# A spectral filter beside a gated MLP on one core: the fifth column class joins the other four on VectorE, tile 3's statistics move to ScalarE, and the warm-up reads a constant

## The chip, the core and the metric

The kernel runs on one core of one Trainium2 chip. The core's engines run side by side and wait for each other through semaphores: TensorE multiplies matrices into PSUM (eight banks), VectorE and ScalarE work on elements and move results from PSUM to SBUF, GpSimd does small element work, and the sync engine issues transfers. The metric is the time of one execution on the device in microseconds (us), as the median of several runs. The profile's span is a little shorter, since it begins with the first instruction and ends with the last.

## The reference, cut to what matters

The input x has 2048 rows of 640 numbers in bf16. Three things are added:

```
xn  = layernorm(x)                              # over the 640 columns
A   = irfft2(rfft2(xn) * (w_r + 1j * w_i))      # over rows and columns; weights 2048 x 321
B   = ((xn @ w_gate) * (xn @ w_up)) @ w_down    # 640 -> 1536 -> 640
out = x + A + B
```

A is a product in the frequency domain: a two-dimensional real Fourier transform, a multiplication by 2048 x 321 complex weights, and the transform back. B is a gated MLP without a nonlinearity.

## The kernel before

Everything lies in one SBUF arena, cut into 16 tiles of 128 rows. The work falls into five stages that overlap.

1. *Layer norm and transposes.* Tiles 0 to 5 get their statistics on VectorE (`bn_stats`, lines 756 and 765), tiles 6 to 15 on ScalarE as a sum and a sum of squares (lines 738 and 747). Tiles 0 to 3 are transposed on TensorE (line 818), the others by transfers. Ahead of it TensorE runs 40 warm-up matmuls and later ten fill matmuls on a small buffer that VectorE sets to zero (lines 696, 709, 720).
2. *The first product of B (GU).* For 12 blocks of 128 hidden columns and for gate and up, five matmuls of 512 columns each (line 948; for the first tiles in smaller pieces, line 968). ScalarE or VectorE moves the result out of PSUM (lines 684 and 685, the copy helper that all evictions share), and VectorE multiplies gate and up (lines 984 and 985, called H). These units are also used as TensorE's filling further down.
3. *The first half of the transform.* VectorE does a radix-10 step over the columns of each tile (lines 860 to 895), TensorE the radix-64 step over rows (line 908, R).
4. *The stage that the change rewrites.* It goes over t = 0 to 15, two frequency groups q of 128 rows each. The 321 column frequencies fall into five classes by their rest modulo 5: four classes of 64 columns and a fifth, the multiples of 5, of 65 columns.
   - D (line 1025): two times five matmuls give real and imaginary parts by columns; eD evicts them in two pieces of 64 partitions each.
   - C (line 1045): two matmuls of 321 columns finish the row transform. Partitions 0 to 63 now hold real parts, 64 to 127 imaginary parts.
   - WM on VectorE: products with w_r and with w_i. Four instructions (line 1062) cover the four classes and go to the buffer PR, two (line 1068) cover the fifth class and go to the buffer Y5.
   - SM, after every second t (lines 1089 and 1090): differences and sums of these products, which complete the complex product for the four classes, go to the buffer L.
   - JA and JB (emitted through line 685 or 684, and through line 1101 or 684): copies of one half of the partitions to the other, one of them with the sign changed, so that L also holds i times the product. They may run on ScalarE or VectorE.
   - NS on GpSimd (lines 1077 to 1079): for the fifth class, two copies and a negation inside Y5.
   - IA (lines 1116 and 1118): the first inverse step for one q. Four matmuls of 64 columns, one for each class, read their weights from L at a step of four elements. The fifth class takes two matmuls that accumulate in PSUM, one for the products with w_r and one for those with w_i, with two different tables (`ti[..., 0]` and `ti[..., 1]`): there TensorE, not VectorE, completes the complex product. eIA evicts to SBUF.
5. *The inverse transform and the second product of B.* I (line 1147) is the inverse over columns on TensorE, V on VectorE the inverse radix-10 step (lines 1171 to 1204). ACC (line 1224) multiplies the hidden values with w_down into PSUM in two halves of 320 columns for each tile, 12 matmuls each, in pieces of five, four and three; IV (line 1236) adds the spectral part into the same bank; FIN adds x and the result is stored (lines 1245 and 1263).

The order of the work is written out. The kernel describes each piece of work as a task with its engine, the buffers it reads and writes and its PSUM bank. A long list, `_PLAN`, says in which order each engine takes the tasks, which engine takes those that may run on two, and which bank they use. A small function replays the list, finds which semaphores each task must wait for, and emits the instructions. Each engine takes its tasks strictly in this order. The numbers of nanoseconds that stand beside the tasks in the code are what the list was planned with; they do nothing on the chip.

The inverse tables TI lie under the w_down rows in the arena, so these rows can be loaded only once the IA that read the tables are done.

Of the kernel before, what the change touches and what calls it, by code (L numbers as in the profile page):

```python
# [255 lines left out]
def _build_tables():  # L256
# [65 lines left out]
    ti = np.zeros((128, _NQ, 2, 64), np.float64)  # L322
    for q in range(_NQ):
        k = _rows(q, npm, nk1)
        ph = two_pi * ((s1[:, None] * k[None, :]) % _S) / _S
        c = np.exp(-1j * ph)
        pm = np.broadcast_to(npm[None, :], (64, 64))
        f = np.where(ck == 1, np.where(pm == 1, -1j, 1j), 1.0 + 0j)
        if q == 0:
            f = (ck == pm).astype(np.complex128)  # L330
        fm = c * f
        im = (np.conj(c) * f / _S).T
        tf[0:64, q, n_re] = fm.real
        tf[0:64, q, n_im] = fm.imag
        tf[64:128, q, n_re] = -fm.imag
        tf[64:128, q, n_im] = fm.real
        ti[n_re, q, 0] = im.real
        ti[n_im, q, 0] = -im.imag
        ti[n_re, q, 1] = im.imag
        ti[n_im, q, 1] = im.real  # L340
# [21 lines left out]
_WD_LOADS = ((7, 12), (0, 2), (2, 4), (4, 6), (6, 7))  # L362
_FT_ORDER = (7, 8, 9, 10, 11, 0, 1, 2, 3, 4, 5, 6)
# [4 lines left out]
_LP = 321  # L368
_YS = 1090
_NY = 3  # L370
# [5 lines left out]
def _d_mm(n):  # L376
    return max(n, 64) / 2.4 + 2.5
# [22 lines left out]
def _d_act(n):  # L400
# [4 lines left out]
    (12, 4, -1), (0, 1, -1), (13, 4, -1), (176, 1, -1), (175, 4, -1), (8, 2, -1), (19, 2, -1), (9, 3, -1), (177, 4, -1),  # L405
    (18, 2, -1), (20, 2, -1), (11, 0, 0), (23, 2, -1), (21, 1, -1), (22, 2, -1), (24, 2, -1), (29, 2, -1), (25, 0, 2),
    (28, 2, -1), (26, 1, -1), (27, 2, -1), (178, 4, -1), (10, 0, 4), (14, 4, -1), (30, 2, -1), (33, 2, -1), (31, 1, -1),
    (32, 2, -1), (187, 0, 5), (34, 2, -1), (185, 0, 4), (188, 1, -1), (35, 0, 6), (15, 4, -1), (37, 2, -1), (192, 0, 5),
    (190, 0, 0), (186, 1, -1), (189, 2, -1), (38, 2, -1), (179, 4, -1), (36, 1, -1), (39, 2, -1), (180, 4, -1), (181, 4, -1),
    (197, 0, 1), (40, 2, -1), (48, 2, -1), (41, 1, -1), (43, 2, -1), (42, 2, -1), (193, 1, -1), (195, 0, 2), (44, 2, -1),  # L410
    (47, 2, -1), (202, 0, 3), (200, 0, 4), (182, 4, -1), (191, 1, -1), (196, 1, -1), (198, 1, -1), (49, 2, -1), (50, 1, -1),
    (16, 4, -1), (194, 2, -1), (201, 1, -1), (45, 0, 2), (52, 2, -1), (51, 2, -1), (183, 4, -1), (53, 2, -1), (207, 0, 6),
    (46, 1, -1), (184, 4, -1), (199, 2, -1), (118, 2, -1), (54, 0, 7), (205, 0, 2), (1, 4, -1), (203, 1, -1), (204, 2, -1),
    (55, 1, -1), (210, 0, 3), (212, 0, 7), (217, 0, 5), (208, 1, -1), (17, 4, -1), (215, 0, 4), (119, 2, -1), (206, 1, -1),
    (209, 2, -1), (120, 2, -1), (56, 2, -1), (211, 1, -1), (60, 2, -1), (59, 2, -1), (2, 4, -1), (3, 4, -1), (57, 2, -1),
    (68, 1, -1), (69, 1, -1), (213, 1, -1), (220, 0, 0), (121, 2, -1), (4, 4, -1), (58, 2, -1), (70, 1, -1), (216, 1, -1),
    (61, 2, -1), (218, 1, -1), (62, 1, -1), (122, 2, -1), (63, 2, -1), (222, 0, 1), (5, 4, -1), (214, 2, -1), (64, 2, -1),
    (125, 0, 2), (221, 1, -1), (71, 1, -1), (223, 1, -1), (123, 0, 6), (126, 1, -1), (219, 2, -1), (227, 0, 4), (127, 2, -1),
    (232, 0, 5), (225, 0, 0), (72, 1, -1), (230, 0, 1), (224, 2, -1), (128, 2, -1), (6, 4, -1), (7, 4, -1), (228, 1, -1),
    (66, 2, -1), (78, 1, -1), (79, 1, -1), (237, 0, 4), (226, 1, -1), (129, 2, -1), (235, 0, 0), (73, 2, -1), (80, 1, -1),  # L420
    (233, 1, -1), (229, 2, -1), (81, 1, -1), (130, 2, -1), (231, 1, -1), (82, 1, -1), (240, 0, 5), (76, 2, -1), (131, 2, -1),
    (238, 1, -1), (134, 0, 2), (74, 2, -1), (236, 1, -1), (83, 2, -1), (234, 2, -1), (242, 0, 4), (84, 2, -1), (65, 4, -1),
    (245, 0, 1), (67, 4, -1), (241, 1, -1), (75, 4, -1), (88, 1, -1), (77, 4, -1), (239, 2, -1), (135, 1, -1), (252, 0, 0),
    (247, 0, 5), (136, 2, -1), (243, 1, -1), (89, 1, -1), (244, 2, -1), (246, 1, -1), (132, 0, 2), (137, 2, -1), (90, 1, -1),
    (91, 1, -1), (86, 2, -1), (248, 1, -1), (250, 0, 1), (249, 2, -1), (255, 0, 4), (92, 1, -1), (98, 1, -1), (251, 1, -1),
    (85, 4, -1), (87, 4, -1), (437, 4, -1), (438, 4, -1), (93, 2, -1), (99, 1, -1), (138, 2, -1), (439, 4, -1), (253, 1, -1),
    (257, 0, 5), (256, 1, -1), (100, 1, -1), (258, 1, -1), (96, 2, -1), (254, 2, -1), (101, 1, -1), (139, 2, -1), (260, 0, 1),
    (262, 0, 0), (267, 0, 4), (94, 2, -1), (263, 1, -1), (133, 1, -1), (102, 1, -1), (261, 1, -1), (259, 2, -1), (140, 2, -1),
    (265, 0, 5), (103, 2, -1), (266, 1, -1), (440, 4, -1), (268, 1, -1), (270, 0, 0), (143, 0, 2), (264, 2, -1), (441, 4, -1),
    (104, 2, -1), (272, 0, 1), (124, 1, -1), (141, 0, 4), (269, 2, -1), (442, 4, -1), (108, 1, -1), (271, 1, -1), (273, 1, -1),  # L430
    (277, 0, 6), (149, 2, -1), (274, 2, -1), (109, 1, -1), (275, 0, 7), (280, 0, 0), (443, 4, -1), (142, 1, -1), (282, 0, 1),
    (444, 4, -1), (276, 1, -1), (278, 1, -1), (147, 0, 4), (281, 1, -1), (445, 4, -1), (145, 0, 6), (150, 2, -1), (446, 4, -1),
    (285, 0, 0), (106, 2, -1), (110, 1, -1), (283, 1, -1), (447, 4, -1), (146, 1, -1), (111, 1, -1), (287, 0, 1), (279, 2, -1),
    (112, 1, -1), (144, 1, -1), (292, 0, 6), (151, 2, -1), (286, 1, -1), (290, 0, 7), (293, 1, -1), (113, 2, -1), (448, 4, -1),
    (284, 2, -1), (152, 2, -1), (288, 1, -1), (116, 2, -1), (291, 1, -1), (297, 0, 2), (474, 4, -1), (475, 4, -1), (289, 2, -1),
    (476, 4, -1), (295, 0, 3), (114, 2, -1), (153, 2, -1), (302, 0, 0), (294, 2, -1), (162, 2, -1), (298, 1, -1), (296, 1, -1),
    (95, 4, -1), (97, 4, -1), (105, 4, -1), (299, 2, -1), (303, 1, -1), (154, 0, 6), (148, 1, -1), (107, 4, -1), (300, 0, 1),
    (477, 4, -1), (301, 1, -1), (156, 0, 2), (158, 0, 4), (159, 1, -1), (305, 0, 0), (155, 1, -1), (478, 4, -1), (160, 0, 4),
    (310, 0, 1), (479, 4, -1), (163, 2, -1), (480, 4, -1), (481, 4, -1), (307, 0, 6), (308, 1, -1), (304, 2, -1), (115, 4, -1),
    (312, 0, 7), (306, 1, -1), (164, 2, -1), (315, 0, 6), (317, 0, 0), (309, 2, -1), (313, 1, -1), (157, 1, -1), (311, 1, -1),  # L440
    (165, 2, -1), (316, 1, -1), (320, 0, 1), (318, 1, -1), (166, 2, -1), (322, 0, 0), (173, 0, 2), (314, 2, -1), (161, 1, -1),
    (167, 0, 6), (323, 2, -1), (321, 1, -1), (169, 0, 4), (174, 2, -1), (168, 1, -1), (325, 0, 1), (171, 0, 6), (170, 1, -1),
    (172, 1, -1), (327, 0, 0), (326, 2, -1), (451, 0, 1), (319, 2, -1), (324, 2, -1), (456, 0, 2), (328, 1, -1), (117, 4, -1),
    (449, 0, 3), (452, 2, -1), (458, 0, 4), (330, 0, 5), (435, 4, -1), (482, 0, 6), (450, 1, -1), (457, 1, -1), (436, 4, -1),
    (459, 2, -1), (705, 4, -1), (507, 4, -1), (508, 4, -1), (453, 0, 0), (509, 4, -1), (337, 0, 7), (510, 4, -1), (329, 2, -1),
    (460, 0, 2), (491, 0, 4), (511, 4, -1), (483, 1, -1), (512, 4, -1), (332, 0, 6), (331, 1, -1), (492, 1, -1), (515, 0, 5),
    (338, 1, -1), (454, 2, -1), (333, 1, -1), (516, 1, -1), (461, 2, -1), (335, 0, 0), (484, 0, 1), (455, 3, -1), (513, 4, -1),
    (340, 0, 4), (514, 4, -1), (485, 1, -1), (463, 2, -1), (342, 0, 5), (486, 0, 6), (522, 0, 1), (334, 2, -1), (336, 1, -1),
    (465, 2, -1), (540, 4, -1), (464, 1, -1), (489, 0, 0), (347, 0, 2), (541, 4, -1), (466, 0, 3), (462, 3, -1), (343, 1, -1),
    (487, 2, -1), (490, 1, -1), (468, 0, 5), (517, 0, 0), (493, 0, 6), (467, 1, -1), (523, 1, -1), (339, 2, -1), (345, 0, 3),  # L450
    (494, 2, -1), (496, 2, -1), (488, 3, -1), (542, 4, -1), (543, 4, -1), (352, 0, 1), (544, 4, -1), (545, 4, -1), (518, 1, -1),
# [71 lines left out]
def _build(nc, A_x, A_w_r, A_w_i, B_w_gate, B_w_up, B_w_down, out, opts=None):  # L523
# [3 lines left out]
    with es:  # L527
# [33 lines left out]
        b_sm = alloc("SM", 384)  # L561
        b_gbf = alloc("GBF", 6 * 512)
        b_stat = alloc("STAT", 608)
        b_dum = alloc("DUM", 256)
        b_jk = alloc("JK", 640)

        o_3 = cur[0]
# [780 lines left out]
```

## Time and profile before

| | |
|---|---|
| time, median of 3 runs (lowest to highest) | 199.53 us (199.37 to 200.29) |
| span in the profile | 197.2 us |
| TensorE busy | 192.8 us |
| VectorE busy | 177.8 us |
| ScalarE busy | 138.0 us |
| GpSimd busy | 28.4 us |
| TensorE's clock granted | 1.0 |
| read from HBM, written to it | 18.92 MB, 2.62 MB |

Busy time is the time in which an engine has at least one instruction in work. Matmuls overlap, so a matmul's own duration says little on what it costs TensorE; the distance from its start to the next one's start does. In a group's line, the text before the first bar is the source line, the engine, the operation, what is written and read, its shape and how often it ran; then come the group's busy time in us and the mean of one in ns, and after the second bar the idle time ahead of it and who ended it.

### The profile page before, as it was taken

What the parts mean: (1) busy time and instruction counts of PE and PEld (TensorE: products, weight loads), DVE (VectorE), ACT (ScalarE), POOL (GpSimd) and SP (SyncE); (2) the same over time, 40 slices, a digit from 0 to 9 for tenths busy, and PEclk for the clock granted to TensorE, in tenths of its full rate; (3) what the DMA queues carried; (4) which work ended last, traced back from release to release, by engine and by line L of the source; (5) the groups of instructions that cost most, each with busy time, mean ns of one, the idle gap of its engine ahead of it and who ended that gap; (6) DMA issues with size and microseconds to landing.
All of it is one profiled execution on the core that took longest, in us unless ns stands there. A gap on an engine that the chain in (4) does not pass through costs nothing.

```text
span 197.2 us, 4300 instructions
## 1 busy us (share of the span) xinstructions
PE 192.8 (98%) x1623; PEld 123.5 (63%) x1623; DVE 177.8 (90%) x396; ACT 138.0 (70%) x299; POOL 28.4 (14%) x53
## 2 busy tenths in 40 slices
PE   7999999999999999999999999999999999999995
PEld 7898645444555555555555555457777777777774
DVE  3799999999999989999898998995999999989753
ACT  3378999999965789999999999966414342335220
POOL 0000000000000003544163460760000000000000
PEclk9999999999999999999999999999999999999999
DMA  6999995245548232532552402003400434233412
GB/s 182 307 328 372 389 128 100 47 118 115 130 94 286 97 82 53 134 100 56 120 145 58 119 17 66 2 3 111 122 3 0 136 100 124 75 103 117 149 70 67
DMA packets 29667, 23.78 MB, mean 121 GB/s; under 512 B 10576, under 2 KB 27600, under 8 KB 29520
## 3 DMA queue, kind: packets, MB, share of 16 engines
q1 hardware_dynamic: 28848, 23.16, 42.3%
q10 hardware_dynamic: 800, 0.36, 0.6%
q8 instruction: 13, 0.21, 0.5%
q14 instruction: 6, 0.05, 0.1%
HBM read 18.92 MB, written 2.62 MB: 109 GB/s over the span
## 4 chain that ended last, share of the span: by engine, by line
PE 72%; ACT 13%; DVE 5%; SPq 4%; DMA 4%; issue 1%
PE ps L948 33%; PE ps L1224 26%; ACT arena L684 7%; SPq L678 4%; DMA arena<-in_A_x_dram 4%; ACT arena L747 3%; ACT arena L738 3%; PE ps L1147 2%; PE ps L1236 2%; PE ps L1116 2%; PE ps L1025 2%; PE ps L1045 2%; PE ps L908 2%; DVE arena L1062 1%; DVE arena L685 1%; PE ps L1118 1%
## 5 line engine op out<-in xcount | busy, mean ns | idle before, releaser
L684 ACT ACTIVATE arena<-ps 128x512 bf16<-128x512 f32 (+6 forms) x245 | 118.5, 525 | 49.5 <-PE ps L1236 21.1
L948 PE MATMUL ps<-arena 128*128 128x512 bf16 x420 | 97.5, 379 | 0.3 <-ACT arena L684 0.2
L948 PEld LDWEIGHTS ps<-arena 128*128 128x128 bf16 x420 | 38.7, 98 | 41.6 <-ACT arena L684 1.4
L1224 PE MATMUL ps<-arena 128*128 128x320 bf16 (+2 forms) x396 | 57.2, 295 | 0.0
L1224 PEld LDWEIGHTS ps<-arena 128*128 128x128 bf16 x396 | 37.5, 98 | 13.3
L1077 POOL COPY arena<-arena 128x126 bf16<-128x126 bf16 x16 | 9.3, 582 | 104.4 <-DVE arena L1068 104.4
L1062 DVE TENSOR_TENSOR arena<-ps,arena 128x256 bf16<-128x256 f32 x64 | 22.6, 416 | 1.5 <-PE ps L1045 1.0
L984 DVE TENSOR_TENSOR arena<-arena 128x512 bf16<-128x512 bf16 x42 | 17.8, 424 | 0.7
L968 PE MATMUL ps<-arena 128*128 128x128 bf16 (+1 forms) x160 | 13.9, 246 | 0.4 <-issue 0.3
L968 PEld LDWEIGHTS ps<-arena 128*128 128x128 bf16 x160 | 12.3, 98 | 1.6 <-issue 0.7
L1079 POOL TENSOR_SCALAR arena<-arena 128x130 bf16<-128x130 bf16 x16 | 11.7, 728 | 0.0
L1263 DVE TENSOR_TENSOR arena<-arena 128x640 bf16<-128x640 bf16 x15 | 7.2, 486 | 4.3 <-ACT arena L684 4.1
L685 DVE CAST arena<-ps 128x512 bf16<-128x512 f32 (+3 forms) x15 | 8.4, 578 | 2.4 <-PE ps L1118 1.7
L1025 PEld LDWEIGHTS ps<-arena 128*128 128x128 bf16 x160 | 7.5, 98 | 3.9 <-ACT arena L684 0.7
L1116 PEld LDWEIGHTS ps<-arena 128*128 128x128 bf16 x128 | 7.8, 119 | 3.1 <-issue 0.8
L1025 PE MATMUL ps<-arena 128*128 128x64 bf16 (+1 forms) x160 | 8.7, 193 | 0.3 <-ACT arena L684 0.3
L1078 POOL COPY arena<-arena 128x126 bf16<-128x126 bf16 x16 | 8.6, 538 | 0.0
L1116 PE MATMUL ps<-arena 128*128 128x64 bf16 x128 | 8.4, 199 | 0.1
L747 ACT ACTIVATE arena<-arena 128x640 bf16<-128x640 bf16 x10 | 8.4, 836 | 0.1
L1068 DVE TENSOR_TENSOR arena<-ps,arena 128x130 bf16<-128x130 f32 x32 | 8.0, 293 | 0.0
L860 DVE TENSOR_TENSOR arena<-arena 128x768 f32<-128x768 bf16 (+1 forms) x10 | 7.9, 792 | 0.0
L1236 PE MATMUL ps<-arena 128*128 128x320 bf16 (+2 forms) x33 | 7.6, 295 | 0.0
(65 smaller groups left out, 204.6 us busy)
## 6 DMA issues: line engine op xcount, KB each, us to landing
arena<-in_A_x_dram SPq DMA_DIRECT2D x20, 160.0 KB, 2.8
arena<-in_A_w_r_dram SPq DMA_DIRECT2D x30, 80.2 KB, 2.2
arena<-in_A_w_i_dram SPq DMA_DIRECT2D x30, 80.2 KB, 2.2
out_dram<-arena SPq DMA_DIRECT2D x15, 160.0 KB, 1.8
arena<-in_B_w_gate_dram SPq DMA_DIRECT2D x4, 320.0 KB, 5.5
arena<-in_A_x_dram SPq DMA_DIRECT2D x1, 1280.0 KB, 10.0
arena<-c_tf SPq DMA_DIRECT2D x4, 256.0 KB, 10.2
arena<-c_ti SPq DMA_DIRECT2D x2, 512.0 KB, 5.4
```

Source lines behind the costliest of these rows:

```text
L684: return c.e.activation(dst, src, _ACTF.Copy)
L685: return c.e.tensor_copy(dst, src)
L747: return c.e.activation(v_jk, v_x[:, b, :], _ACTF.Square, scale=-1.0, bias=v_m32[:, b:b + 1], accum_out=v_ss[:, b:b + 1])
L948: ins = c.e.matmul(ps[:, bk, :], v_gw[:, w, j, ft, :], v_xt[:, j, rows], start=(j == 0), stop=(j == 4))
L968: ins = c.e.matmul(ps[:, bk, w * n:(w + 1) * n], v_gw[:, w, j, ft, :], v_xt[:, j, rows], start=(j == 0), stop=(j == 4))
L984: return c.e.tensor_tensor(v_ht[:, ft0, rows], v_gbf[:, rr, 0, :], v_gbf[:, rr, 1, :], _OP.mult)
L1025: ins = c.e.matmul(ps[:, bk, k * 64:k * 64 + n], v_uq[:, k, t, :], v_fd[:, k * 128 + w * n: k * 128 + w * n + n], start=True, stop=True)
L1062: c.e.tensor_tensor(dst, xh, wv, _OP.mult)
L1079: return c.e.tensor_scalar(yg[:, :, 128:193], yg[:, :, 256:321], -1.0, None, _OP.mult)
L1116: c.e.matmul(ps[:, bk, 64 * k:64 * k + 64], yl[:, k:512:4], v_ti[:, q, 0, :], start=True, stop=True)
L1224: ins = c.e.matmul(ps[:, bk, 0:sl3.stop - sl3.start], v_ht[:, ft, a * 128:(a + 1) * 128], v_wd[:, ft, sl3], start=(ft == _FT_ORDER[0]), st ...
L1236: return c.e.matmul(ps[:, bank_of(own), 0:sl3.stop - sl3.start], v_sm[:, 2, :], v_v[:, a, sl3], start=False, stop=True)
```

## The change

Three edits, with a new order list for everything.

1. *The fifth class as a fifth row.* Its products go into PR beside those of the other four classes, interleaved by four frequencies at a step of four elements (lines of `d5` below). SM then covers five rows of 264 elements instead of four of 256, JA and JB five rows of 256 instead of four, and IA reads the fifth class from L as it reads the others: one matmul instead of two, with the same table. Y5, the NS tasks on GpSimd and half of the table TI go. A pad task on GpSimd sets the edges of the rows to zero once. Since TI is half as long, more of w_down can be loaded ahead (rows 4 to 11 of 12, before 7 to 11), and ACC takes its blocks in the order that fits.
2. *Tile 3's statistics* are computed on ScalarE instead of VectorE.
3. *The warm-up* and fill matmuls read a constant of ones that the program's preamble has set up, instead of a buffer that VectorE has to clear; the fill has 12 matmuls instead of ten.

The new `_PLAN` changes the order on every engine and which of the two engines takes some evictions and copies; it is left out here.

```diff
-        ti[n_re, q, 0] = im.real
-        ti[n_im, q, 0] = -im.imag
-        ti[n_re, q, 1] = im.imag
-        ti[n_im, q, 1] = im.real
+        ti[n_re, q] = im.real
+        ti[n_im, q] = -im.imag
...
-_WD_LOADS = ((7, 12), (0, 2), (2, 4), (4, 6), (6, 7))
-_FT_ORDER = (7, 8, 9, 10, 11, 0, 1, 2, 3, 4, 5, 6)
+_WD_LOADS = ((4, 8), (8, 12), (0, 2), (2, 4))
+_FT_ORDER = (4, 5, 6, 7, 8, 9, 10, 11, 0, 1, 2, 3)
...
-        def em_wz(c):
-            return c.e.memset(v_dum, 0.0)
-        T("warm_zero", "dve", 150.0, em_wz, writes=[(b_dum, None)], prio=-1.0)
...
-        nfill = opts.get("nfill", 10)
+        nfill = opts.get("nfill", 12)
...
-                ins = c.e.matmul(ps[:, bk + (i % 2), (i % 4) * 128:(i % 4 + 1) * 128], v_dum[:, 0:128],
-                                 v_dum[:, 128:256], start=True, stop=True)
+                ins = c.e.matmul(ps[:, bk + (i % 2), (i % 4) * 128:(i % 4 + 1) * 128], v_one, v_one, start=True, stop=True)
...
-        aset = set(opts.get("act_set", ())) | set(range(opts.get("act_stats", 6), 16))
+        aset = set(opts.get("act_set", (3,))) | set(range(opts.get("act_stats", 6), 16))
...
+        def em_pad(c):
+            c.e.memset(v_pr[:, :, 0:4, 0:4], 0.0)
+            return c.e.memset(v_pr[:, :, :, 260:264], 0.0)
+        T("pad", "pool", 200.0, em_pad, writes=[(b_pr, ("r", 2, 3))], prio=9.9)
...
-                        dst = v_pr[:, w, 2 * pb:2 * pb + 2].rearrange("p g (h m k) -> p h g m k", h=2, k=4)[:, h]
+                        dst = v_pr[:, w, 2 * pb:2 * pb + 2, 4:260].rearrange("p g (h m k) -> p h g m k", h=2, k=4)[:, h]
...
-                    ins = c.e.tensor_tensor(d5[w], ps[:, bk:bk + 2, 256:321], wt[:, w, :, 0:321:5], _OP.mult)
+                    d5 = v_pr[:, w, 4, 0:260].rearrange("p (n g) -> p g n", g=4)[:, 2 * pb:2 * pb + 2]
+                    ins = c.e.tensor_tensor(d5, ps[:, bk:bk + 2, 256:321], wt[:, w, :, 0:321:5], _OP.mult)
...
-            T("NS_%d" % t, "pool", 1180.0, em_ns,
...
-                c.e.tensor_tensor(v_l[0:64, lr, :, 0, :], pa_[0:64], pb_[64:128], _OP.subtract)
-                return c.e.tensor_tensor(v_l[64:128, lr, :, 0, :], pa_[64:128], pb_[0:64], _OP.add)
+                c.e.tensor_tensor(v_l[0:64, lr, :, 0:264], pa_[0:64], pb_[64:128], _OP.subtract)
+                return c.e.tensor_tensor(v_l[64:128, lr, :, 0:264], pa_[64:128], pb_[0:64], _OP.add)
...
-                return copy_on(c, v_l[0:64, lr, :, 1, :], v_l[64:128, lr, :, 0, :])
+                return copy_on(c, v_l[0:64, lr, :, 260:516], v_l[64:128, lr, :, 4:260])
...
-                    for i in range(2):
-                        ins = c.e.matmul(ps[:, bk, 256:320], v_y5[:, yr, g, 128 * i:128 * i + 128], v_ti[:, q, i, :],
-                                         start=(i == 0), stop=(i == 1))
+                    yl, y5 = v_l[:, lr, q % 4, 4:516], v_l[:, lr, 4, q % 4:512]
+                    for k in range(5):
+                        st = yl[:, k:512:4] if k < 4 else y5[:, 0:509:4]
+                        ins = c.e.matmul(ps[:, bk, 64 * k:64 * k + 64], st, v_ti[:, q, :], start=True, stop=True)
```

## The prediction

> **What bounds the kernel now.** I read the page's first part, then TensorE's timeline for holes, then the stage that the change rewrites.
>
> ```profile
> PE 192.8 (98%) x1623; PEld 123.5 (63%) x1623; DVE 177.8 (90%) x396; ACT 138.0 (70%) x299; POOL 28.4 (14%) x53
> PE 72%; ACT 13%; DVE 5%; SPq 4%; DMA 4%; issue 1%
> ```
>
> TensorE has nearly the whole span, and the chain that ended last stays on it. Busy is not peak, so I looked at starts: a 512-column matmul follows the last after 216 ns (1.08 us per five) almost everywhere. From 5.4 us to the last matmul at 194.7 us the holes over 60 ns add up to 2.7 us: 1.0 us up to 12.3 us, 0.4 us at 39.6 us, 1.3 us in the stage D to IA, none after 135.66 us. So time can come only out of TensorE's work or these 2.7 us.
>
> The stage D to IA (first spectral matmul 71.58 us, first inverse one, line 1147, 135.66 us: 64.08 us) is where the change works. Busy time of its middle, from the first product with the weights to the last swap copy, all engines:
>
> ```profile
> 74.45:133.28 58.83, 58.36 (x541) 32.34 (x539) 55.26 (x148) 55.28 (x122) 28.00 (x48) 1.00 0.28 72
> ```
>
> After the interval and its length the columns are TensorE, its weight loads, VectorE, ScalarE, GpSimd. VectorE and ScalarE are both 94% busy beside a TensorE at 99%: three engines in near balance, VectorE and ScalarE without reserve. The groups that the change touches, mean ns last before the idle time:
>
> ```profile
> L1116 PE MATMUL ps<-arena 128*128 128x64 bf16 x128 | 8.4, 199 | 0.1
> L1118 PE MATMUL ps<-arena 128*128 128x64 bf16 x64 | 6.8, 193 | 0.0
> L1068 DVE TENSOR_TENSOR arena<-ps,arena 128x130 bf16<-128x130 f32 x32 | 8.0, 293 | 0.0
> L1089 DVE TENSOR_TENSOR arena<-arena 64x1024 bf16<-64x1024 bf16 x8 | 5.5, 688 | 0.3
> L1101 DVE TENSOR_SCALAR arena<-arena 64x1024 bf16<-64x1024 bf16 x8 | 3.4, 422 | 0.3
> L684 ACT ACTIVATE arena<-arena 64x1024 bf16<-64x1024 bf16 x3 | 3.2, 1051 | 0.0
> ```
>
> What a matmul costs TensorE is read from starts, since 199 and 193 ns are latency:
>
> ```profile
> 81.43 0.31 PE L1116 MATMUL ps<-arena 128*128 128x64 bf16 x4
> 81.57 0.22 PE L1118 MATMUL ps<-arena 128*128 128x64 bf16 x2
> 81.63 0.30 PE L1116 MATMUL ps<-arena 128*128 128x64 bf16 x4
> 81.77 0.22 PE L1118 MATMUL ps<-arena 128*128 128x64 bf16 x2
> 82.28 0.32 PE L1025 MATMUL ps<-arena 128*128 128x64 bf16 x5 [0.28 <-ACT arena L684]
> ```
>
> Four matmuls of line 1116 take 0.14 us (35 ns each), two of line 1118 0.06 us (30 ns each): a frequency costs 0.20 us. The last line is one of the stage's holes.
>
> [...] The trace has 29 to 30 ns for line 1118, but 35 ns for line 1116, whose weights stand four elements apart (weight load 119 against 98 to 101 ns); the measured number is used. [...] no output of before steps by single elements, though the weight read of line 1068 does, and its 293 ns are the price of a dense one. [...] line 1079 takes 540 to 1183 ns, while line 1089 keeps 687 to 689 ns.
>
> **Part by part.** *TensorE.* Per frequency four matmuls at 35 and two at 30 ns (200) become five with weights four apart (5 x 35 = 175). 32 x 25 ns = 0.8 us less, all of it on the path.
>
> *GpSimd.* The three operations of lines 1077 to 1079, 29.6 us in all, go. GpSimd waited 104.4 us for VectorE and nothing waited for it in the listed waits, so this buys only two GLU products (519 and 529 instead of some 420 ns): 0.2 us. Its new pad writes lie ahead of the first sum and hide behind the tail of the first stage.
>
> *VectorE, sums.* Lines 1089 and 1090 go from 1024 to 5 x 264 = 1320 elements. From 640 elements (line 1263, 485 ns) to 1024 (688 ns) the slope is 0.53 ns per element; 296 more cost 156 ns, x16 = +2.5 us.
>
> *Swap copies.* 1024 to 1280 elements. [...] Twelve instead of 13 lie on VectorE: +0.4 to +1.2 us. ScalarE takes four instead of three, each (601 - 440)/(512 - 320) = 0.84 ns x 256 = 215 ns longer: +1.9 us.
>
> *Fifth products.* Line 1068 now writes every fourth element. [...] I take 0, because the read at a five-element step shows no charge.
>
> *New order.* In the stage, by the two orders of issue, VectorE gives two GLU evictions (685 ns) and three IA evictions (487 ns, about 400 in a queue) to ScalarE and takes one pair of D evictions (2 x 494): -1.4 - 1.2 + 1.0 = -1.6 us; ScalarE +1.5 us or so. A GLU product now stands between products and sum in six of eight pairs, hiding some 0.09 us of hand-over each: -0.5 us. And nine ACC matmuls (136 ns) that filled TensorE before the first inverse matmul now come after it: 1.2 us less for TensorE in the stage, 1.2 us more behind it, where it has no holes.
>
> *Start.* Tile 3's statistics leave VectorE (0.9 + 0.2 us) for ScalarE (740 + 836 ns and two accumulator reads of 0.2 us). VectorE takes two early GLU evictions (0.36 us) for it. On ScalarE the first statistic of tile 3, landed at 9.52 us, now stands ahead of the square root of tile 2, ready at 10.2 us; tile 2's transpose may then come 0.3 us later than 12.01 us. TensorE's large hole there, at 8.2 us, ends when the weights land at 8.58 us and stays. The warm-up starts some 0.3 us earlier, since it waits for no memset, and ends before the transpose of tile 0, which waits for data until 5.37 us. I book 0, with 0.3 us either way.
>
> *DMA.* The inverse table halves, to 0.5 MB; the w_down rows under it now reload after the last IA, but the ACC pieces that need them come 5 us later. 0.
>
> *The sum for the stage.* TensorE alone: 64.08 - 1.3 (holes) - 0.8 - 1.2 = 60.8 us. VectorE: 2.87 us to its first product, then 58.83 us now, of which 1.63 us are the waits the timeline names (0.36, 0.17, 0.42, 0.68), so 57.2 us of work; +2.5 +0.4..1.2 -1.6 -0.5 -0.2 makes 57.8 to 58.6 us, 57.3 if the hand-overs close up further. After the last copy four IA, their evictions and the first inverse matmul need 1.85 us (2.38 us now, with fill). So VectorE, without a wait, needs 2.87 + 57.3 + 1.85 = 62.0 us or more: it becomes the bound and TensorE's saving is not reached in full. With 0.7 us of waits, under half of now because the others now wait for it, the stage takes 62.7 us. That is 1.4 us shorter, and the 1.2 us of ACC come behind it: -0.2 us, 199.4 us.
>
> **The rivals.** *A, the forecast:* TensorE's gain is used up by VectorE; 199.4 us. For it: 94% on VectorE, +2.5 us of certain work. Against it: the new order may fit better than such sums see.
>
> *B, faster:* ScalarE's and VectorE's queues close up so far that TensorE sets the stage but for 0.5 us: 61.5 us, -2.6 + 1.2 = -1.4, 198.1 us. For it: evictions follow each other on ScalarE 0.1 us closer than their durations say, so its 94% overstates; against it: VectorE's work alone is above 61.5 us.
>
> *C, slower:* the odd row split is paid and waits stay at 1.6 us: 2.87 + 58.6 + 1.6 + 1.85 = 64.9 us, +0.8 + 1.2 = 201.5 us. For it: the same engines hand over in the same pattern. Against it: waits on TensorE shrink when it has less to do.
>
> *D, slower:* the stepped write costs its upper price: A + 2.7 = 202.1 us. Against it: the stepped read is free.
>
> **Numbers.** Chances: A 0.42, B 0.34, C 0.15, D 0.09. The 0.5% bounds are 198.5 and 200.5 us. B is mostly below (0.30) and A at its lower edge (0.06): faster 0.36. C and D are above but for 0.02, A at its upper edge (0.03): slower 0.25. Same: 0.39. The range 197.8 to 201.5 us leaves out the better end of B, half of C and all of D.
>
> **What would show it.** Right: lines of the sums at 0.84 us, IA at 0.17 to 0.18 us per frequency, VectorE above 95% in the stage, TensorE's holes there grown beyond 1.3 us and ended by VectorE or ScalarE. The fifth products still at 293 ns clear D; a swap copy at 0.49 us clears the odd split, 0.55 us shows it. Wrong: a stage of 61.5 us or less without holes is B. A later transpose of tile 2 would show the start's cost.

## The result, and the profile after

The changed kernel takes 201.33 us (median of 4 runs, 201.20 to 201.46), the kernel before 199.70 us beside it (199.37 to 200.29). The ratio is 1.0078, 95% interval 1.0052 to 1.0105: 0.8% slower, 1.6 us. I had forecast no change, 199.4 us.

First the page of the kernel after: busy time by engine, then the chain that ended last.

```profile
PE 192.2 (96%) x1577; PEld 122.5 (61%) x1593; DVE 182.0 (91%) x390; ACT 142.0 (71%) x305; POOL 0.5 (0%) x7
PE 70%; DVE 23%; issue 4%; DMA 1%; DVEq 0%
```

VectorE and ScalarE gain 4 us each, which leaves their shares of the span almost as they were; GpSimd's 28 us are gone. The chain tells more. VectorE had 5% of it and now has 23%. Inside the stage, from 71.5 to 136 us, the chain spent about 8 us on VectorE before and spends about 42 us there now, and nearly all of its "issue" lies between two VectorE instructions. (ScalarE's 13% before say little of the stage: about 23 us of it lie ahead of 40 us.) The stretch from the first product to the last swap copy says the same (columns as in the prediction):

```profile
74.32:135.27 60.95, 58.31 (x494) 31.50 (x501) 59.56 (x145) 58.39 (x126) 0.00 (x0) 1.00 0.25 65
```

It was 58.83 us and is 60.95 us. VectorE is 98% busy in it (59.56 us, before 55.26), and the trace names no wait of VectorE between these points, where it named 1.63 us before. TensorE has the named waits instead, all for VectorE (line waited at, releaser, total, times, longest). In the kernel after, line 936 is the first product of B, 1037 is C, 1098 is IA; on VectorE 1058 are the fifth products, 1072 is the second sum, and 678 is the copy helper:

```profile
PE ps L1037 <- DVE arena L1072: 0.7, 2, 0.4
PE ps L936 <- DVE arena L1058: 0.5, 2, 0.3
PE ps L1098 <- DVE arena L1058: 0.3, 1, 0.3
PE ps L1098 <- DVE arena L678: 0.2, 1, 0.2
```

From TensorE's first spectral matmul to the first inverse one the stage takes 136.81 - 71.45 = 65.36 us, before 64.09: +1.27 us. From there to the last matmul it takes 60.27 us, before 59.05: +1.22 us. The second part has no holes before or after; it is the nine ACC matmuls that moved behind (9 x 136 ns). Together they are 2.5 us, and the spans say the same (199.6 us against 197.2), but the time grows by 1.6 us only.

The difference lies outside the span. Time less span is 2.1 to 2.5 us in every run of the kernel before and of its two variants below, and 1.75 to 2.05 us in every run of the kernel after and its variants. So the change wins about 0.5 us ahead of the first instruction or behind the last one. The constant warm-up alone does not bring it (2.3 us, last experiment); what does, no run here shows. Ratios of times to the kernel before have this 0.5 us in them, stages have not. In the twelve traces whose stages are used here the first spectral matmul starts anywhere from 71.24 to 71.75 us, so a stage is measured within one trace.

The groups that the change touched, mean of one in ns ahead of the second bar:

```profile
L1058 DVE TENSOR_TENSOR arena<-ps,arena 128x130 bf16<-128x130 f32 x32 | 11.9, 473 | 0.0
L1071 DVE TENSOR_TENSOR arena<-arena 64x1320 bf16<-64x1320 bf16 x8 | 6.7, 842 | 0.3
L1083 DVE TENSOR_SCALAR arena<-arena 64x1280 bf16<-64x1280 bf16 x6 | 3.3, 553 | 0.2
L1082 ACT ACTIVATE arena<-arena 64x1280 bf16<-64x1280 bf16 x2 | 2.5, 1264 | 0.0
L1098 PE MATMUL ps<-arena 128*128 128x64 bf16 x160 | 8.9, 198 | 0.5 <-DVE arena L1058 0.3
```

The sums (842 ns, 844 foretold) and ScalarE's copies (1264, 1266 foretold) are where the working put them. VectorE's copies take 553 ns, the 0.55 us that was to show the odd split (five rows as the outermost count of a copy). The fifth products are not where I had them: 473 instead of 293 ns.

A duration is not yet a cost, since VectorE often starts an instruction before the one ahead has ended (in the first fence below at 82.13 us, where the fifth products last until 82.21). VectorE's timeline of one pair of column blocks shows the cost; before (start, length, line):

```profile
80.39 1.42 DVE L1062 TENSOR_TENSOR arena<-ps,arena 128x256 bf16<-128x256 f32 x4
81.72 0.49 DVE L1068 TENSOR_TENSOR arena<-ps,arena 128x130 bf16<-128x130 f32 x2
82.13 0.42 DVE L984 TENSOR_TENSOR arena<-arena 128x512 bf16<-128x512 bf16 x1
```

and after:

```profile
81.34 1.42 DVE L1054 TENSOR_TENSOR arena<-ps,arena 128x256 bf16<-128x256 f32 x4
82.67 0.74 DVE L1058 TENSOR_TENSOR arena<-ps,arena 128x130 bf16<-128x130 f32 x2
83.22 1.44 DVE L1054 TENSOR_TENSOR arena<-ps,arena 128x256 bf16<-128x256 f32 x4
```

Two fifth products hold the queue for 82.13 - 81.72 = 0.41 us before, and for 83.22 - 82.67 = 0.55 us after. So it is for 12 of the 16 t of the kernel after, 0.13 us more each on average. For the other four a sum or a swap copy comes next, and in the trace it starts 0.03 to 0.04 us after the products have ended. There more of the duration counts; after:

```profile
106.14 0.76 DVE L1058 TENSOR_TENSOR arena<-ps,arena 128x130 bf16<-128x130 f32 x2
106.93 0.55 DVE L1083 TENSOR_SCALAR arena<-arena 64x1280 bf16<-64x1280 bf16 x1
```

and at the same place of the version below that writes every second element:

```profile
105.13 0.51 DVE L1058 TENSOR_TENSOR arena<-ps,arena 128x130 bf16<-128x130 f32 x2
105.67 0.55 DVE L1083 TENSOR_SCALAR arena<-arena 64x1280 bf16<-64x1280 bf16 x1
```

0.79 us against 0.54. The sum is 12 x 0.13 + 4 x 0.25 = 2.6 us, on an engine that has no named wait left to hide it in.

### The profile page after: what moved, and what is told of

The parts are those of the page before. It is cut to its first block, busy times and chain, and to the rows that moved or that the text cites. A ratio compares the mean times of both kernels' runs of the same rounds, so it can differ in the third digit from the quotient of the medians.

```text
span 199.6 us, 4180 instructions
## 1 busy us (share of the span) xinstructions
PE 192.2 (96%) x1577; PEld 122.5 (61%) x1593; DVE 182.0 (91%) x390; ACT 142.0 (71%) x305; POOL 0.5 (0%) x7
## 4 chain that ended last, share of the span: by engine, by line
PE 70%; DVE 23%; issue 4%; DMA 1%; DVEq 0%
PE ps L936 28%; PE ps L1203 26%; DVE arena L1054 8%; PE ps L956 7%; DVE arena L1058 4%; DVE arena L1072 3%; DVE arena L678 2%; DVE arena L972 2%; PE ps L896 2%; PE ps L1126 2%; PE ps L1215 2%; PE ps L1098 1%; DMA arena<-in_A_x_dram 1%; DVE arena L1083 1%; DVE arena L744 1%
## 5 line engine op out<-in xcount | busy, mean ns | idle before, releaser
L936 PE MATMUL ps<-arena 128*128 128x512 bf16 x404 | 95.4, 379 | 1.4 <-DVE arena L1058 0.5
L1058 DVE TENSOR_TENSOR arena<-ps,arena 128x130 bf16<-128x130 f32 x32 | 11.9, 473 | 0.0
L1098 PE MATMUL ps<-arena 128*128 128x64 bf16 x160 | 8.9, 198 | 0.5 <-DVE arena L1058 0.3
L735 ACT ACTIVATE arena<-arena 128x640 bf16<-128x640 bf16 x11 | 9.2, 837 | 0.0
L678 DVE CAST arena<-ps 64x321 bf16<-64x321 f32 (+4 forms) x14 | 7.3, 531 | 1.4 <-PE ps L1017 0.9
L726 ACT ACTIVATE arena<-arena 128x640 bf16<-128x640 bf16 x11 | 8.1, 740 | 0.3 <-DMA arena<-in_A_x_dram 0.3
L1037 PE MATMUL ps<-arena 128*128 128x321 bf16 x32 | 7.0, 299 | 1.1 <-DVE arena L1072 0.7
L744 DVE BATCH_NORM_STATS2 arena<-arena 128x6 f32<-128x320 bf16 x10 | 4.3, 484 | 3.8 <-DMA arena<-in_A_x_dram 3.7
```

Of the source, the lines that this page charges most:

```text
L678: return c.e.tensor_copy(dst, src)
L735: return c.e.activation(v_jk, v_x[:, b, :], _ACTF.Square, scale=-1.0, bias=v_m32[:, b:b + 1], accum_out=v_ss[:, b:b + 1])
L936: ins = c.e.matmul(ps[:, bk, :], v_gw[:, w, j, ft, :], v_xt[:, j, rows], start=(j == 0), stop=(j == 4))
L1058: ins = c.e.tensor_tensor(d5, ps[:, bk:bk + 2, 256:321], wt[:, w, :, 0:321:5], _OP.mult)
L1098: ins = c.e.matmul(ps[:, bk, 64 * k:64 * k + 64], st, v_ti[:, q, :], start=True, stop=True)
```

## The experiments

Theory S: the stepped write of the fifth products, which I priced at nothing, turns VectorE into the bound and is the loss. Rivals: theory W, the rest of VectorE's added work (longer sums, odd row split); theory O, the new order and the ACC matmuls behind the stage. All ratios are to the kernel before, run beside each kernel (199.54 to 199.64 us).

**Dense fifth products.** The output's fifth class is out of order; nothing else changes.

```diff
-  d5 = v_pr[:, w, 4, 0:260].rearrange("p (n g) -> p g n", g=4)[:, 2 * pb:2 * pb + 2]
+  d5 = v_pr[:, w, 4, 0:260].rearrange("p (g n) -> p g n", g=4)[:, 2 * pb:2 * pb + 2]
```

> The changed kernel, but the fifth products are written densely (65 elements in a row for each frequency) instead of at every fourth element; everything else, order and amounts, is kept. The inverse step then reads the fifth class in the wrong order, so that part of the output is not the reference's. Theory S (the stepped write is the main cost): the fifth product falls from 473 to about 293 ns, VectorE's stretch from the first product to the last copy (60.95 us) by 16 x 0.13 = 2.1 us to about 58.9 us, and the time from 201.3 to about 199.3 us (199.0 to 199.8). Theory W (the wider sums and copies are the main cost): the stretch is then held by them; less than 0.7 us is won, 200.6 us or more. Theory O (the new order costs the time): VectorE waits instead, time 201 us or more.

Measured 199.34 us, ratio 0.9990 (0.9983 to 0.9998). The whole loss of time goes with the step, although the sums, the copies and the order are those of the kernel after. Inside the span 2.0 of some 2.3 us go: the median spans are 199.5 us after, 197.5 dense and 197.2 before. In the one trace of this version the span is 1135 us, with 170.1 us of VectorE's waits put down to C on TensorE (line 1037), so no stage is read from it; the fifth products are as foretold:

```profile
L1058 DVE TENSOR_TENSOR arena<-ps,arena 128x130 bf16<-128x130 f32 x32 | 7.8, 284 | 0.0
```

**The step put into the kernel before.** The fifth class is not the reference's here.

```diff
-  d5 = [d5[:, :, 256 * w:256 * w + 65] for w in range(2)]
+  d5 = [d5[:, :, w:w + 257:4] for w in range(2)]
```

> The kernel before, with one thing added: its fifth products are written at every fourth element of the same buffer instead of densely (the later steps read that buffer as before, so the fifth class of the output is not the reference's). Theory S: the fifth product rises from 293 to about 470 ns, VectorE's stretch by 2.1 us less what its 1.6 us of waits take up, so 0.5 to 2.1 us more: 200.1 to 201.8 us. Theories W and O: 199.7 us, within 0.3 us.

Measured 200.77 us, ratio 1.0057 (1.0044 to 1.0070). The old order and the old sums with the stepped write alone give three quarters of the loss of time. In the stretch from first product to last copy VectorE's busy time grows by 2.6 us (57.90 against 55.26), and the stretch by 1.26 us, since VectorE idled for 3.6 us there before and for 2.2 us now. The line of that kernel:

```profile
L1068 DVE TENSOR_TENSOR arena<-ps,arena 128x130 bf16<-128x130 f32 x32 | 11.9, 473 | 0.0
```

The same 473 ns in a different order: it is the access that costs. Theory O falls with these two runs as the main cause.

**VectorE's swap copies split evenly.** Five rows of 256 become two halves of five rows of 128. Of the two copies the diff shows the one with the sign; the other is edited alike.

```diff
+  def halves(x):
+      return x.rearrange("p g (h n) -> p h g n", h=2)
...
-  return c.e.tensor_scalar(dst, src, -1.0, None, _OP.mult)
+  return c.e.tensor_scalar(halves(dst), halves(src), -1.0, None, _OP.mult)
```

> The changed kernel, but the swap copies on VectorE are written with an outermost count of two (two halves of 128 in each of five rows) instead of five; same elements, same result. If the odd row count is what makes them 553 ns instead of some 490 ns, they fall to about 490 ns, VectorE's stretch by 12 x 0.065 = 0.8 us, and since VectorE is never idle in it, the time by the same: about 200.5 us (200.2 to 200.9). If their width alone sets them, nothing moves: 553 ns, 201.3 us. Theory O expects 201.3 us in both cases.

Measured 200.71 us, ratio 1.0054 (1.0041 to 1.0066). The copies:

```profile
L678 DVE COPY arena<-arena 64x1280 bf16<-64x1280 bf16 x6 | 2.9, 491 | 0.2
```

491 instead of 555 ns, and the stretch from first product to last copy falls from 60.95 to 60.18 us, which is 12 x 64 ns = 0.77 us. The time falls by 0.6 us, but the intervals of the two ratios overlap; the trace is the better witness. Theory W is real in this part, and it is the smaller one.

**Pairs: the two frequencies of a bank innermost,** so that two elements (4 bytes) are written side by side at every 8 bytes.

```diff
-  d5 = ....rearrange("p (n g) -> p g n", g=4)[:, 2 * pb:2 * pb + 2]
-  ins = c.e.tensor_tensor(d5, ps[:, bk:bk + 2, 256:321], wt[:, w, :, 0:321:5], _OP.mult)
+  d5 = ....rearrange("p (n g) -> p n g", g=4)[:, :, 2 * pb:2 * pb + 2]
+  ins = c.e.tensor_tensor(d5, ps[:, bk:bk + 2, 256:321].rearrange("p g n -> p n g"),
+                          wt[:, w, :, 0:321:5].rearrange("p g n -> p n g"), _OP.mult)
```

> The changed kernel, but each fifth product runs with the two frequencies as its innermost loop: the same elements go to the same places, as 65 pairs of neighbours (4 bytes each, 8 bytes apart) instead of two passes of single elements 8 bytes apart; same result. If the price is for single 2-byte writes, it is gone: about 293 ns and 199.3 us, as with dense writes. If it is for every jump, half of it stays: about 380 ns, 200.3 us. The read from PSUM now alternates between two banks, which may cost something of its own; then it is 473 ns or more and 201.3 us or more.

Measured 199.62 us, ratio 1.0002 (0.9993 to 1.0011), with the line

```profile
L1058 DVE TENSOR_TENSOR arena<-ps,arena 128x130 bf16<-128x130 f32 x32 | 9.1, 325 | 0.0
```

Same elements, same places, another order of visiting them: 325 instead of 473 ns, and the loss of time is gone. In the queue two of them still take 0.48 us (82.30 to 82.78 us in the trace), where dense ones take 0.41.

**Every second element** instead of every fourth; the fifth class comes out in another order.

```diff
-  d5 = v_pr[:, w, 4, 0:260].rearrange("p (n g) -> p g n", g=4)[:, 2 * pb:2 * pb + 2]
+  d5 = v_pr[:, w, 4, 0:260].rearrange("p (h n g) -> p h g n", h=2, g=2)[:, pb]
```

> The kernel after, with the fifth products written at every second element (4 bytes apart) in place of every fourth (8 bytes apart); the order within the fifth row changes, so the fifth class of the output is not the reference's. Theory distance (the price of the stepped write grows with the step): a fifth product lasts between 293 and 473 ns, about 350 to 400, and the time lies at 200.0 to 200.7 us. Rival any step (a write that is not dense costs the full price): 473 ns and 201.3 us. Rival free (two elements in one 8-byte group are as good as dense): 293 ns and 199.4 us.

Measured 199.17 us, ratio 0.9980 (0.9968 to 0.9993). The line and a pair in the timeline:

```profile
L1058 DVE TENSOR_TENSOR arena<-ps,arena 128x130 bf16<-128x130 f32 x32 | 8.1, 302 | 0.0
```

```profile
82.42 0.50 DVE L1058 TENSOR_TENSOR arena<-ps,arena 128x130 bf16<-128x130 f32 x2
82.83 1.41 DVE L1054 TENSOR_TENSOR arena<-ps,arena 128x256 bf16<-128x256 f32 x4
```

302 ns and 0.41 us per two, as dense. The middle expectation (a price that grows with the step) misses, and so does the one of a full price for any step. A product takes 302 ns at a step of 4 bytes (dense 284 to 293) and 473 at 8 bytes. VectorE has only 2% of this version's chain; ScalarE has 10%, all of it in the stage.

**Pairs and the even split together,** the two edits above.

> The kernel after, with both of the two repairs: the fifth products written with the two frequencies of a bank innermost, and the swap copies of VectorE split into an even outermost dimension. Theory VectorE (the stage between the first products and the last swap copy is as long as VectorE's own work there, so every nanosecond taken off it counts): the two gains seen alone, 1.7 and 0.6 us, add up, about 199.0 us, some 0.5 us under the kernel before. Rival TensorE (the stage is already at TensorE's floor once the products are repaired): the second repair brings nothing more, 199.5 to 199.7 us.

Measured 199.25 us, ratio 0.9984 (0.9977 to 0.9990). This is the only version with the whole computation that beats both kernels: by 0.16%, against the 0.25% hoped for. The chain that ended last:

```profile
PE 94%; DVE 2%; DMA 1%; issue 1%; ACT 1%; DVEq 0%
```

VectorE has left the stage's chain. In the stretch to the last copy the two gains add up but for 0.1 us (0.77 and 1.82, together 2.51 us); in the stage 0.27 us is missing (0.76 and 1.78, together 2.27 us), because the first inverse matmul comes 1.78 instead of 1.54 us after the last copy. Another limit is near. The span is no shorter than before (medians 197.4 and 197.3 us), so the lead over the kernel before comes from the 0.5 us outside it.

**Every second element and the even split.**

> The kernel after, with the fifth products at every second element (dense price in the earlier run; the order of the fifth class in the output is not the reference's) and VectorE's swap copies split evenly. It has 1.2 us less on VectorE than the version with pairs and the even split (32 times 38 ns in the spacing of the fifth products), which stood at 199.25 us, and 0.8 us less than the one with every second element and the odd split, 199.17 us. Theory VectorE still sets the stage: 198.2 to 198.6 us. Theory floor (about 63 us from first D to first inverse matmul, set by TensorE and its small waits): 199.0 to 199.2 us.

Measured 199.16 us, ratio 0.9976 (0.9969 to 0.9984): no better than with the odd split (0.9980). The stretch to the last copy does shorten, from 58.31 to 57.91 us, but the first inverse matmul then comes 2.35 instead of 1.96 us after that copy. That is the time which the theory of a floor expected; its chain has ScalarE with 10% too, so the floor need not be TensorE's alone.

**Fifth row left out of sums and copies,** fifth products dense (the fifth class is wrong by that; its row in L is zeroed once). It has 1056-element sums, 705 ns, not the 1024 that the expectation speaks of.

```diff
-  c.e.tensor_tensor(v_l[0:64, lr, :, 0:264], pa_[0:64], pb_[64:128], _OP.subtract)
+  c.e.tensor_tensor(v_l[0:64, lr, 0:4, 0:264], pa_[0:64, 0:4], pb_[64:128, 0:4], _OP.subtract)
...
-  dst, src = v_l[64:128, lr, :, 260:516], v_l[0:64, lr, :, 4:260]
+  dst, src = v_l[64:128, lr, 0:4, 260:516], v_l[0:64, lr, 0:4, 4:260]
```

> The kernel after, with the fifth products written densely and the fifth row left out of the sums and of the swap copies (their result for the fifth class is not the reference's; the row of the L store is zeroed once), so that VectorE has 1024-element sums and four-row copies as before the change while TensorE keeps the 33 matmuls per pair. Theory VectorE: the sums give back 16 times 156 ns = 2.5 us and the copies about 1.2 us, until TensorE's own 60.8 us sets the stage: 197.0 to 198.3 us. Rival (TensorE or a fixed cost of the new order sets the stage already with dense products): not under 199.0 us.

Measured 198.72 us, ratio 0.9966 (0.9954 to 0.9978): between the two expectations, outside both. Against the dense version VectorE has 16 x 137 ns + 12 x 132 ns = 3.8 us less to do, ScalarE's four copies lose 0.8 us as well (1052 instead of 1268 ns each), and the ratio falls by 0.0024, 0.5 us. VectorE now waits (two of its lines), and the chain passes through ScalarE in the stage (the first fence is VectorE's waits, the second the chain's shares):

```profile
DVE arena L678 <- PE ps L1099: 1.3, 1, 1.3
DVE arena L972 <- ACT arena L677: 1.3, 2, 0.9
```

```profile
PE 85%; ACT 10%; DMA 1%; DVE 1%; issue 1%
```

**ScalarE's four swap copies given to VectorE,** first in the version just shown (its edit is four entries of the order list), then in the one with pairs and the even split. The second number of an entry is the engine, 1 for ScalarE and 2 for VectorE.

```diff
-  (462, 1, -1) ... (523, 1, -1) ... (648, 1, -1), (647, 1, -1)
+  (462, 2, -1) ... (523, 2, -1) ... (648, 2, -1), (647, 2, -1)
```

> The version that leaves the fifth row out of sums and copies and writes the fifth products densely (198.7 us; its fifth class is not the reference's), with the four swap copies of ScalarE given to VectorE, which had over 4 us of waits there: ScalarE loses 4 us of work, VectorE gains 1.7 us. It asks what is left when VectorE no longer sets the stage. If ScalarE's evictions share the bound with TensorE, the stage shortens by 0.3 to 1 us: 197.8 to 198.4 us. If TensorE alone sets it: 198.6 to 198.9 us. If VectorE is bound again by where the copies stand in its queue: over 199.2 us.

Measured 198.28 us, ratio 0.9942 (0.9922 to 0.9963). ScalarE now waits 3.0 us for TensorE's GLU matmuls:

```profile
ACT arena L677 <- PE ps L936: 3.0, 4, 1.6
```

> The version with pairs and the even split (199.25 us), with the four swap copies of ScalarE given to VectorE: ScalarE loses 4 times 1.27 us = 5 us, VectorE gains 4 times 0.49 = 2.0 us. If VectorE sets the stage: 200.3 to 201.3 us. If it has slack by now and ScalarE's copies held up evictions: 198.6 to 199.2 us.

Measured 201.00 us, ratio 1.0073 (1.0056 to 1.0091), and the chain is back on VectorE:

```profile
PE 71%; DVE 21%; issue 3%; ACT 2%; DMA 1%; DVEq 0%
```

The same exchange gains 0.4 us where VectorE has room and loses 1.8 us of the 2.0 us added where it has none. The loss is clear. The gain is less so: the intervals of the two ratios overlap (0.9954 to 0.9978, 0.9922 to 0.9963), though the stage is 0.55 us shorter too. With four rows ScalarE shares the bound with TensorE, as its part of the chain says (10%, then 5%). With five rows VectorE has almost no room even after both repairs. The exchange was not tried with every second element and the even split, where VectorE waits for 2.2 us in the stage and ScalarE has 10% of the chain.

**The constant warm-up alone,** in the kernel before.

```diff
+  v_one = nc.const_aps.tensor(1.0, (128, 128), _BF)
-  ins = c.e.matmul(..., v_dum[:, 0:128], v_dum[:, 128:256], start=True, stop=True)
+  ins = c.e.matmul(..., v_one, v_one, start=True, stop=True)
```

> The kernel before with the constant warm-up alone: the warm-up and fill matmuls read a constant of the program in place of the memory that GpSimd clears. My prediction took the start at 0 with bounds of 0.3 us either way; the traces put the first matmul of the stage 0.12 us earlier in the kernel after. If the warm-up does that, 199.4 us, a ratio of 0.999 to 1.000; if the 0.12 us comes from elsewhere (tile 3 statistics), no change at all[...].

Measured 199.63 us, ratio 1.0003 (0.9995 to 1.0010): no difference, and the granted clock is 1.000 in its trace. (The cleared buffer is cleared by VectorE, not by GpSimd as my expectation says.) The 0.1 us by which the stage starts earlier in the kernel after is within what the first spectral matmul moves between kernels with the same start (71.24 us with pairs, 71.75 us with every second element and the even split).

All but the dense version, which has no stage to read, and the warm-up alone, in one table, the kernel before first and the others by falling ratio: us from the first product to the last swap copy, and from the first spectral to the first inverse matmul.

```
kernel                                  ratio    to last copy   stage
before                                  1        58.82          64.09
after                                   1.0078   60.95          65.36
after, pairs + even, all copies VectorE 1.0073   60.56          64.98
before + stepped write                  1.0057   60.08          65.08
after, even split                       1.0054   60.18          64.60
after, pairs                            1.0002   59.13          63.58
after, pairs + even split               0.9984   58.44          63.09
after, every second element             0.9980   58.31          63.14
after, every second + even split        0.9976   57.91          63.13
after, dense, four rows                 0.9966   57.06          62.67
after, dense, four rows, copies VectorE 0.9942   57.50          62.12
```

(Versions of after carry 1.22 us more behind the stage than those of before, and 0.5 us less outside the span.)

## Why the prediction was wrong, step by step

**The step that failed: "Fifth products ... I take 0, because the read at a five-element step shows no charge."** A read was taken as the price of a write. The write costs 180 ns of duration each (473 against 293 ns), and 0.07 us of queue, or 0.12 us where a sum or a copy follows: 2.6 us in the stage. The 2.7 us of case D were my estimate and rested on no trace. Over 32 products they are 84 ns each, too little for a duration and too much for most of the queue; that the sum meets the 2.6 us is luck. Why a write at every fourth element takes so long is not shown. The runs give the durations alone: 284 to 293 ns dense, 302 at every second element, 324 to 327 for pairs at 8 bytes, 473 to 474 at every fourth element. The read of the weights at every fifth element is another matter. That read shows no charge, as I said: line 1245 of the kernel before has dense products of PSUM and SBUF, 292 ns for 128 elements (one instruction), beside 293 ns for the 130 of line 1068.

**VectorE's sum was otherwise right in its upper end.** With the odd split paid its terms make 58.6 us; the missing 2.6 us make 61.2, and the trace has 60.95. Without the step (every second element) it has 58.31 us, waits included. So the sums and copies were sized well, the new order as a whole fits, and the waits vanished as I had said they would, even to nothing. The forecast itself used 57.3 us: the lower price of the copies, and hand-overs closing up by another 0.5 us, which the runs don't show. Those 1.3 us were missing too, and 0.7 us of waits and 0.3 us behind the last copy (1.54 instead of 1.85) that were booked and did not come made up for most of it. So of the 2.7 us by which the stage was missed (65.36 against 62.7) the step is nearly all.

**The odd split** was left open: the +0.4 to +1.2 us for the swap copies were my estimate, and no trace of before shows either end. It is paid: 553 ns against 422 for four rows, 131 ns more, and 12 x 553 - 13 x 422 ns = 1.15 us is the upper end. The even split takes 489 to 491 ns, 67 to 69 ns above four rows, and 12 x 489 - 13 x 422 ns = 0.38 us is the lower end. Why the odd count takes longer is not shown. Case C had it right in this, and lands near the measured time (201.5 us) for another reason: its 1.6 us of waits did not stay.

**TensorE and the part behind the stage.** IA costs 34 ns a matmul, 0.17 us a frequency, as predicted, and the nine ACC matmuls came behind the stage at 1.22 us. The 0.8 us are real, but no version with five rows collects them in the span. VectorE's added work (2.5 us of sums, 0.4 us or more of copies) is one reason, as the loss by 2.0 us more of it shows; that ScalarE's four longer copies are another is argued from the chain only. Case A's picture, a gain of TensorE used up by VectorE, is what pairs and the even split show: 199.25 us where A said 199.4, with the 0.5 us outside the span in it, which A didn't have.

**Start and DMA at 0** hold within what the traces can tell: tile 2's transpose starts at 12.02 us (12.01 before), so the feared 0.3 us didn't come. The 0.2 us from GpSimd's silence fit as well: the longest GLU product of the stage, 529 ns before, is 462 ns now. The tile 3 statistics were not tried alone.

**The choice of chances.** I gave case D 9% on the ground that the stepped read is free (293 ns beside 292 for a dense product). The two sides of this operation, read and write, needed two prices (293 and 473 ns), and 32 instructions on the engine that I had just named the new bound deserved the bad one.

What stays open: why the dense version, with the four rows and the copies moved, keeps 1.3 us of stage above TensorE's own work (62.12 us against the 60.8 of the prediction), in six holes of 0.1 to 0.5 us of which the trace names 0.5 us; and what wins the 0.5 us outside the span.

## What to carry to other kernels

An engine that your own sum makes the new bound has to be priced at its upper bounds: a layout change that saves another engine 0.8 us was paid with 2.6 us of access pattern. Before giving up on such a layout, change the order in which the elements are visited (inner loop over the neighbours, 473 to 325 ns; even outermost count, 553 to 489 ns): here it took back 2.1 us with the same data in the same places. Read the chain's shares by engine after each edit, inside the stage that you changed; they named the bound (VectorE 23%, then TensorE 94%, then ScalarE 10%) when busy shares hardly moved. And compare span with time: here they disagreed by 0.5 us.

## What the hardware showed that I had not expected

- A VectorE product of 130 bf16 results from PSUM and SBUF: dense 284 to 293 ns, every second element 302, pairs at 8 bytes 325, every fourth element 473. The dense one reads its SBUF input at every fifth element, and that shows no charge (293 ns beside 292 for a dense product of 128).
- Duration overstates that: 180 ns longer each is 70 ns longer in the queue where a product follows, since the end of a fifth product overlaps the next instruction (for 0.08 us in the kernel before, 82.21 against 82.13 us, and for 0.19 us in the kernel after, 83.41 against 83.22), and 120 ns where a sum or a copy follows.
- A matmul of 64 columns follows the last after 29 to 30 ns with weights side by side (line 1118 of the kernel before) and after 34 to 35 ns with weights four elements apart (line 1116 before, line 1098 after). The weight load takes 98 to 101 ns in the first case and 118 to 119 in the second: here a step costs TensorE's loads too.
